# Transposing transfers from unit 3 on instead of unit 5, with a new hand-written order, in a fused gated-recurrence and MLP kernel

## The chip, the cores and the metric

The kernel runs on one core of one Trainium2 chip. The metric is device microseconds of one execution, median of three. All arithmetic is fp32. The engines are TensorE (PE, with its weight loads as PEld), VectorE (DVE), ScalarE (ACT), GpSimd (POOL) and SyncE (SP). SP issues most of the DMAs. [...]

## The reference

```python
def _attn_ref(q, k, v, f_logit):          # (B, H, S, D) = (4, 8, 768, 48)
    f = 1.0 / (1.0 + np.exp(-f_logit))
    state = np.zeros((B, H, D, D))
    for t in range(S):
        state = f[:, :, t, :, None] * state + einsum('bhd,bhe->bhde', k[:, :, t], v[:, :, t])
        y[:, :, t] = einsum('bhd,bhde->bhe', q[:, :, t], state)
    return y
def _moe_ref(x, g_ln, w_ch1, w_ch2):      # x: (4, 768, 384), heads side by side
    xn = (x - mean) / sqrt(var + 1e-6) * g_ln
    return x + maximum(xn @ w_ch1, 0.0) @ w_ch2      # 384 -> 1536 -> 384
```

The inputs q, k and v are normal with deviation 0.1. f_logit is normal with mean 2.0 and deviation 0.5, so a gate f is about 0.88.

## The kernel before

**Units.** The 768 positions are cut into NU = 12 units of T = 64. A unit holds all four batches and eight heads, 256 rows in all. Unit n first goes through attention and then through the MLP, and attention runs ahead of the MLP by one to three units. In attention a unit is turned so that a head's 48 channels lie on the partitions and its 64 positions along the free axis. ACT takes the sigmoid of f into `gates` (L674 to L684). Two scans on DVE then run the product of gates over the 64 positions, from the end (`after`, L652) and from the start (`upto`, L664). DVE multiplies k by `after` (kh) and q by `upto` (qh). PE makes the scores, the part carried from the state, the values, and the sum that goes into the next state (`chunk`).

**Two ways to turn a tile.** For n < DIRECT (5 before) the tiles of f, q, k and kh are turned by PE against the identity (`across` L640, `do_kt` L765), eight 128x128 transposes for each tensor, and ACT or DVE reads the result from PSUM. For n >= DIRECT three steps do it. `split` (L426) has ACT cut half a tile into two 16-bit planes and POOL issue its store to DRAM. `transfer` (L440) has SP issue a transposing DMA back. The turned f and the turned q land in the same tile, `turned`. The turned k lands in the tile that held raw q before. Raw q of such a unit is loaded into k's tile (`raw_of`, L417). `do_gates` (L679) then reads `turned` for f, and `do_q` (L715) reads `turned` for q.

**The order is text.** START is the order of the first units and UNIT is repeated for m = 3 to 11, with n = m+1, o = m+2, p = m+3 and z = m+4. `run` (L1035) carries out one token after another in the order written, and every engine's queue and every dependence between two accesses of a tile follows from it. The tokens:

- `a3.gates` and so on: one stage of attention of unit 3; a stage already done is passed over
- `m2`: the next step of unit 2's MLP
- `l4k`: load k of unit 4; `p4k0`: split half 0 of it; `x4k`: its transposing transfer. K is kh, whose transfer is issued by `a4.kt`
- `f`, `r`, `w`: fetch, read and write one piece of the weights, which arrive as 64-bit numbers
- `t`, `T`, `u`, `U`: mixtures of the weights on DVE or (capitals) POOL
- `d`: an idle matmul; `s2`, `y3`: sums that the MLP's fast matrix products need

**MLP.** Units 0 to 2 compute the first layer plainly (L956) and units 3 to 11 by a scheme of 15 block products (L894). Units 0 and 1 compute the second layer plainly (L966) and the others by seven products (L985).

**The check at the end.** `do_q` keeps in `least` (L717) the smallest product of gates over the 64 positions of any channel of any unit (`total`, L661, not below 1e-30). After UNIT of m = 9 the minimum is taken, and at m = 10 `small` is set to 1 if it lies under LEAST = 1e-12 (L1078). After the last unit every engine loads `small` into a register (L1083) and branches on it (L1084). If it is 1, `general_path` (L19 to L296) computes the entire output again from the inputs, without a division by products of gates. It is a loop over 4 batches, and in it a loop over 3 stretches of 256 positions. Each pass loads its four tensors in eight transfers, turns f, q and k by PE, builds the scores by seven doublings of a block (L153 to L187), each with 16 matmuls, two products in place and a predicated copy, and then runs its MLP plainly (36 and 24 matmuls of 256 and 384 columns). Nothing of one pass lies beside the next.

Of the kernel before, what the change touches and what calls it, by code (L numbers as in the profile page):

```python
# [8 lines left out]
FP32 = mybir.dt.float32  # L9
# [289 lines left out]


START = """
l0k a0.gates l0q f d d a0.after d r l0v a0.kx
a0.upto f a0.kept l1f a0.k l1k d a0.q f a0.carried a0.scores a0.causal
a0.values l1q w d r d a0.stats f a0.kt a1.gates w
a0.norm d a1.after l1v a0.chunk a0.turn f r a0.state a1.upto m0 d
a1.kept w a1.kx f a1.k m0 a1.q f r a1.kt r w
a1.carried d a1.scores a1.causal f l2k f l2v f w m0 a1.values
l2f r r a1.stats a1.chunk w m0 a1.norm m0 a1.turn r m0
m1 r w m1 r w w f l2q w m1
f m1 a1.state a2.gates a2.after r m1 a2.kx m0 m0 r w  # L310
a2.k l3k w a2.upto a2.kept m1 a2.q m0 m0 m0 a2.carried l3q
m0 a2.scores l3v a2.causal U m1 a2.values a2.stats l3f a2.norm m1
m1 m1 a3.gates m1 a2.kt m1 a2.turn a2.chunk a3.kx m2 l4f a3.after
U a3.k a3.upto U T m2 a2.state m2 a3.q a3.kept m2 a3.carried
a3.scores a3.kt U U l4v l4k a4.gates a3.causal U U U t
U a3.values a3.chunk l4q T l5v a4.after m2 l5f U a3.stats m2
a4.kx U l5k a3.norm s2 m2 p5f0 a3.state m2 a4.k U m2
p5f1 m2 a4.kt a3.turn u l6f x5f p5k0 a4.upto a4.q p5k1
y3 l5q a5.gates m2 m2 a4.kept m2
"""  # L320
UNIT = """
m{m} a{o}.after a{n}.kt m{m} a{n}.carried p{o}q0 a{n}.scores m{m} p{o}q1 a{n}.causal m{m} m{m}
l{p}k m{m} m{m} a{o}.upto a{n}.values x{o}q x{o}k m{m} a{n}.stats p{p}f0 p{p}f1 m{m}
m{m} a{n}.chunk m{m} a{n}.norm m{m} m{m} m{m} m{m} s{m} m{m} p{p}k0
p{p}k1 l{p}q m{m} a{o}.q m{m} x{p}f a{n}.turn a{o}.k l{p}v p{o}K0 a{p}.gates m{m}
a{n}.state l{z}f a{o}.kept m{m} y{n} m{m} m{m} p{o}K1
"""


# [1 line left out]
def kernel(  # L331
# [21 lines left out]
    P = 128  # L353
    T = 64
# [3 lines left out]
    NS = 2 * GA  # L358
# [8 lines left out]
    LEAST = 1e-12  # L367
    PLAIN = 2
    FIRST = 3
    DIRECT = 5  # L370
    PIECE = 768

    outer = ctx.enter_context(tc.tile_pool(name="outer", bufs=1))
# [10 lines left out]
    work = fast.enter_context(tc.tile_pool(name="work", bufs=1))  # L384
# [17 lines left out]
    for name, fill in (("f", 40.0), ("q", 0.0), ("k", 0.0)):  # L402
        t = consts.tile([P, G, H, 64], FP32, name=f"{name}raw")
# [7 lines left out]
    turned = {}  # L411
# [3 lines left out]
    def raw_of(n, name):  # L415

        return wide_heads["k" if n >= DIRECT and name == "q" else name]  # L417

# [7 lines left out]
    def split(n, name, g):  # L426

        if n >= NU or n < DIRECT:
            return
# [10 lines left out]
    def transfer(n, name):  # L440

        if n >= NU or n < DIRECT:
            return
        if not turned:
            turned["k"] = wide_heads["q"].rearrange("p g h e -> p (g h e)").rearrange(
                "p (s t) -> p s t", t=T)
            turned["f"] = turned["q"] = late["pool"].tile([P, NS, T], FP32, name="turned")
        transposed(turned[name].rearrange("p (g s) t -> p g (s t)", g=G), n, name)

    def transposed(dst, n, name):  # L450
        there = halved.pop((n, name))
        to = dst.rearrange("p g c -> p (g c)").bitcast(U16)
        nc.sync.dma_start_transpose(out=to.rearrange("p (a r) -> p a r", a=GA),
                                    in_=there.rearrange("p two g c -> (p two) (g c)"))
# [130 lines left out]
    late = {}  # L585
# [42 lines left out]
    def attention(n):  # L628
# [7 lines left out]
        def new(name, shape, **kw):  # L636
            at[name] = work.tile(shape, FP32, tag=name, name=f"{name}{n}", **kw)
            return at[name]

        def across(src, g):  # L640

            pt = one_bank(f"tr{n}")
            for a in range(NP):
                nc.tensor.transpose(pt[:, a * P:(a + 1) * P],  # L644
                                    src[:, g, 2 * a:2 * a + 2].rearrange("p h e -> p (h e)"),
                                    ident)
            return pt.rearrange("p (s t) -> p s t", t=T)
# [20 lines left out]
        def times(dst, pts, by):  # L668
            for g, pt in enumerate(pts):
                segs = slice(g * HS, (g + 1) * HS)  # L670
                nc.vector.tensor_tensor(out=dst[:, segs], in0=pt, in1=by[:, segs, 1:E1],
                                        op=ALU.mult)

        def do_gates():  # L674
            new("after", [P, NS, E1])
            new("upto", [P, NS, E1])
            new("total", [P, NS], bufs=2)
            if n >= DIRECT:
                nc.scalar.activation(out=gv[:, :, 1:E1], in_=turned["f"], func=AF.Sigmoid)  # L679
# [17 lines left out]
        def do_k_across():  # L697
            if n < DIRECT:
                at["pk"] = [across(loaded[n, "k"], g) for g in range(G)]

        def do_k():
            kh = new("kh", [P, NS, T])
            if n < DIRECT:
                times(kh, at["pk"], at["after"])
# [330 lines left out]
    def run(plan):  # L1035
        for token in plan.split():
            kind, rest = token[0], token[1:]
            if kind == "a":
                n, stage = rest.split(".")
                if int(n) >= NU:  # L1040
                    continue
                if "a" + n not in running:
                    running["a" + n] = attention(int(n))
                running["a" + n].pop(stage, bool)()
            elif kind == "m":
                if token not in running:
                    running[token] = mlp(int(rest))
                next(running[token])
            elif kind == "l":
                load(int(rest[:-1]), rest[-1])  # L1050
            elif kind == "p":
                split(int(rest[:-2]), rest[-2], int(rest[-1]))
            elif kind == "x":
                transfer(int(rest[:-1]), rest[-1])
            elif kind == "s":
                sums(int(rest))
            elif kind == "y":
                if FIRST <= int(rest) < NU:
                    sums_of_x(int(rest))
            else:  # L1060
                {"r": read, "w": write, "f": fetch, "t": mix, "d": idle,
                 "T": lambda: mix(nc.gpsimd), "u": mix_step,
                 "U": lambda: mix_step(nc.gpsimd)}[token]()
# [53 lines left out]
```

## Time and profile before

| | |
|---|---|
| median of three runs | 444.21 us (443.25 to 448.19) |
| the profiled execution | 446.42 us, its span 444.6 us |
| TensorE busy | 425.5 us (96%) |
| VectorE, ScalarE, GpSimd busy | 332.8, 201.7, 146.3 us |
| granted TensorE clock | 1.000 |
| transposing transfers | 28, four for each of units 5 to 11 |
| transposes of f, q, k, kh on PE | 160, 32 for each of units 0 to 4 |
| one repeated unit | about 33 us |

Busy time of each engine by stretch of the execution, in us:

| stretch | length | PE | DVE | ACT | POOL | DMA share |
|---|---|---|---|---|---|---|
| 0 to 26 | 26.0 | 16.11 | 19.78 | 10.44 | 8.23 | 0.95 |
| 26 to 100 | 74.0 | 72.24 | 55.71 | 31.51 | 26.59 | 0.68 |
| 100 to 150 | 50.0 | 49.96 | 35.81 | 18.66 | 29.45 | 0.53 |
| 150 to 183.5 | 33.5 | 33.50 | 28.23 | 18.01 | 10.41 | 0.75 |
| 217 to 250 | 33.0 | 33.00 | 27.32 | 18.78 | 11.14 | 0.85 |
| 412 to 445 | 33.0 | 28.08 | 13.22 | 6.83 | 3.11 | 0.09 |

A row is a stretch of the span, and a number is how long that engine had an instruction in work in it. Of the lines of `general_path` the trace holds no instruction.

### The profile page before, as it was taken

To read this page: it belongs to the slowest core of one execution; us is meant where nothing else is said; L and a number is where in the kernel's file an instruction comes from. 1 tells how busy PE (TensorE), PEld (TensorE's weight loads), DVE (VectorE), ACT (ScalarE), POOL (GpSimd) and SP (SyncE) were. 2 spreads that over 40 slices of the span, in tenths; PEclk is the share of its full clock that TensorE was granted. 3 is DMA by queue.
4 is the path that set the end of the run, shared out by engine and by line. 5 is a ranking of instruction groups with operands and counts; after the bars stand their busy time and mean duration, and the time that the engine had idled before them with its cause. 6 is when DMAs were issued, how large, how long until landed. Compare 5 with 4: busy or idle time off the path is not lost.

```text
span 444.6 us, 12876 instructions
## 1 busy us (share of the span) xinstructions
PE 425.5 (96%) x5427; PEld 393.0 (88%) x5427; DVE 332.8 (75%) x528; ACT 201.7 (45%) x345; POOL 146.3 (33%) x165
## 2 busy tenths in 40 slices
PE   5789999999999999999999999999999999999995
PEld 4567787667899999989999989989999999999995
DVE  5897979443878988878888878878888878566461
ACT  2456772013244556456456556556555444151320
POOL 2214444139815123323324323323324214102011
PEclk9999999999999999999999999999999999999999
DMA  8996893241737759897978897898988871400001
GB/s 139 205 230 211 211 249 76 53 91 37 130 60 151 175 98 217 197 158 205 201 128 230 207 192 163 199 194 167 204 190 160 180 148 43 111 1 19 20 2 39
DMA packets 175630, 63.29 MB, mean 142 GB/s; under 512 B 162512, under 2 KB 168144, under 8 KB 175568
## 3 DMA queue, kind: packets, MB, share of 16 engines
q1 hardware_dynamic: 169312, 47.34, 55.7%
q0 software_dynamic: 4480, 14.68, 9.7%
q8 instruction: 44, 0.72, 0.7%
q10 hardware_dynamic: 1776, 0.40, 0.5%
q14 instruction: 18, 0.15, 0.1%
HBM read 28.31 MB, written 19.40 MB: 107 GB/s over the span
## 4 chain that ended last, share of the span: by engine, by line
PE 83%; DVE 6%; DMA 4%; issue 3%; POOL 2%; SPq 1%; ACT 1%; POOLq 0%; ACTq 0%
PE pp L985 28%; PE ph L956 11%; PE bx L894 10%; PE by L894 7%; PE po L966 7%; DMA kt<-Khalves 3%; PE bz L894 3%; PE shared L750 3%; PE py L736 2%; PE tr L644 2%; PE py L778 2%; PE shared L809 2%; PE bv L894 2%; PE bw L894 2%; PE xp L842 2%
## 5 line engine op out<-in xcount | busy, mean ns | idle before, releaser
L905 ACT ACTIVATE h<-h 128x512 f32<-128x512 f32 x45 | 28.1, 630 | 52.2 <-DVE h L902 48.0
L956 PE MATMUL ph<-xt,w 128*128 128x256 f32 x216 | 48.7, 381 | 0.6 <-ACT xt L844 0.6
L956 PEld LDWEIGHTS ph<-xt,w 128*128 128x128 f32 x216 | 40.3, 190 | 6.3 <-issue 0.8
L985 PE MATMUL pp<-mixed,h 128*128 128x192 f32 x240 | 42.4, 327 | 0.0
L985 PE MATMUL pp<-mixed,s 128*128 128x192 f32 x240 | 42.0, 326 | 0.0
L985 PE MATMUL pp<-w,h 128*128 128x192 f32 x240 | 40.7, 326 | 0.0
L985 PEld LDWEIGHTS pp<-mixed,h 128*128 128x128 f32 x240 | 39.5, 190 | 0.3 <-ACT xt L844 0.3
L985 PEld LDWEIGHTS pp<-mixed,s 128*128 128x128 f32 x240 | 39.1, 190 | 0.0
L985 PEld LDWEIGHTS pp<-w,h 128*128 128x128 f32 x240 | 38.8, 190 | 0.0
L993 POOL TENSOR_TENSOR p1x<-p,x 128x192 f32<-128x192 f32 x10 | 13.1, 1312 | 66.5 <-ACT p L1000 66.5
L902 DVE TENSOR_TENSOR h<-h,bx 128x512 f32<-128x512 f32 x27 | 18.6, 687 | 21.1 <-PE bx L894 21.1
L966 PE MATMUL po<-w,h 128*128 128x384 f32 x96 | 32.4, 489 | 0.0
L652 DVE TENSOR_TENSOR_SCAN after<-gates,ends 128x1040 f32<-128x1040 f32 (+1 forms) x13 | 29.1, 2236 | 4.0 <-ACT gates L684 3.3
L797 POOL TENSOR_SCALAR rstd<-mv 128x2 f32<-128x2 f32 x12 | 3.1, 261 | 84.6 <-DVE mv L796 84.6
L664 DVE TENSOR_TENSOR_SCAN upto<-gates,starts 128x1040 f32<-128x1040 f32 (+1 forms) x13 | 30.0, 2305 | 0.4
L844 ACT ACTIVATE xt<-xp,gain 128x128 f32<-128x128 f32 x72 | 20.1, 375 | 21.1 <-PE xp L842 21.0
L894 PE MATMUL bx<-y,v 128*128 128x128 f32 x216 | 29.4, 279 | 0.0
L902 DVE TENSOR_TENSOR h<-h,by 128x512 f32<-128x512 f32 x36 | 24.5, 682 | 5.2 <-PE by L894 5.0
L966 PEld LDWEIGHTS po<-w,h 128*128 128x128 f32 x96 | 17.7, 190 | 11.0
L894 PEld LDWEIGHTS bx<-y,v 128*128 128x128 f32 x216 | 26.2, 192 | 0.5
L958 ACT ACTIVATE h<-ph 128x512 f32<-128x512 f32 x18 | 10.8, 597 | 29.5 <-PE ph L956 29.4
L556 POOL TENSOR_TENSOR w<-w_0upper,w_0units 128x768 int32<-128x768 int32 x7 | 12.7, 1818 | 30.7 <-DVE w_0upper L554 26.3
(162 smaller groups left out, 954.0 us busy)
## 6 DMA issues: line engine op xcount, KB each, us to landing
w_0words<-in_moe_w_ch_dram SPq DMA_DIRECT2D x7, 768.0 KB, 6.3
kraw<-in_k_dram SPq DMA_DIRECT2D x48, 96.0 KB, 3.8
v<-in_v_dram SPq DMA_DIRECT2D x48, 96.0 KB, 3.8
fraw<-in_f_logit_dram SPq DMA_DIRECT2D x46, 96.0 KB, 3.5
fhalves<-fplanes POOLq DMA_DIRECT2D x14, 256.0 KB, 5.3
khalves<-kplanes POOLq DMA_DIRECT2D x14, 256.0 KB, 3.5
qhalves<-qplanes POOLq DMA_DIRECT2D x14, 256.0 KB, 3.5
Khalves<-Kplanes POOLq DMA_DIRECT2D x14, 256.0 KB, 3.5
```

The lines of the kernel that those rows point to most:

```text
L556: nc.gpsimd.tensor_tensor(out=to.bitcast(I32), in0=upper, in1=units, op=ALU.add)
L652: nc.vector.tensor_tensor_scan(out=at["after"].rearrange(flat)[:, c0:c1][:, ::-1], data0=gt[:, c0 + 1:c1 + 1][:, ::-1], data1=ends.rearran ...
L664: nc.vector.tensor_tensor_scan(out=at["upto"].rearrange(flat)[:, c0:c1], data0=gt[:, c0:c1], data1=starts.rearrange(flat)[:, c0:c1], initi ...
L750: nc.tensor.matmul(ps[half(b), r, e], lhsT=kh[head_rows(r), seg], rhs=qh[head_rows(r), seg], start=True, stop=True)
L844: nc.scalar.mul(out=xt[:, m, g * P:(g + 1) * P], in_=pt[:, m], mul=gain[:, m:m + 1])
L894: nc.tensor.matmul(banks[bank][:, i], lhsT=right[:, i * P:(i + 1) * P], rhs=left, start=new and i == 0, stop=True, skip_group_check=True)
L902: nc.vector.tensor_tensor(out=out[to], in0=out[to], in1=bank, op=op)
L905: nc.scalar.activation(out=out[to], in_=out[to] if bank is None else bank, func=AF.Relu)
L956: nc.tensor.matmul(ph[:, j], lhsT=w1[:, m, (i + j) * P:(i + j + 1) * P], rhs=xt[:, m], start=m == 0, stop=m == KD - 1)
L966: nc.tensor.matmul(po, lhsT=h[:, i, g * P:(g + 1) * P], rhs=w2[:, i], start=i == 0, stop=i == KF - 1)
L985: nc.tensor.matmul(pp, lhsT=a[:, i], rhs=b[:, i], start=i == 0, stop=i == KH - 1)
L993: engine.tensor_tensor(out=to, in0=x1, in1=x2, op=op)
```

## The change

DIRECT becomes 3, so f, q, k and kh of units 3 and 4 are split and transferred as well. START gets the splits and transfers of units 3 and 4 (sixteen `p`, six `x` and two transfers in `a3.kt` and `a4.kt`) and loses `a3.kx`, `a4.kx` and `a4.kt`, of which the last is now done in UNIT. Both orders are new. The tile `turned` comes from another pool, since it is needed before the later pool exists.

```diff
 START = """
-l0k a0.gates l0q f d d a0.after d r l0v a0.kx
-a0.upto f a0.kept l1f a0.k l1k d a0.q f a0.carried a0.scores a0.causal
-a0.values l1q w d r d a0.stats f a0.kt a1.gates w
...
-m1 m1 a3.gates m1 a2.kt m1 a2.turn a2.chunk a3.kx m2 l4f a3.after
-U a3.k a3.upto U T m2 a2.state m2 a3.q a3.kept m2 a3.carried
-a3.scores a3.kt U U l4v l4k a4.gates a3.causal U U U t
-U a3.values a3.chunk l4q T l5v a4.after m2 l5f U a3.stats m2
-a4.kx U l5k a3.norm s2 m2 p5f0 a3.state m2 a4.k U m2
-p5f1 m2 a4.kt a3.turn u l6f x5f p5k0 a4.upto a4.q p5k1
-y3 l5q a5.gates m2 m2 a4.kept m2
+a0.upto a0.after f l0k d d a0.gates l0q l0v r d a0.kx f l1f a0.kept a0.k l1k d d a0.q f
+a0.scores a0.causal a0.carried f a0.kt l1q w a0.values r d d a0.stats a1.gates f w
...
+a2.gates a2.after m1 a2.kx m0 r m0 w a2.k l3f r w l3k a2.upto a2.kept m1 m0 p3f0 p3f1
+a2.q m0 m0 x3f a2.carried p3k1 l3q p3k0 a2.scores m1 l3v a2.causal a2.values a2.stats
+a3.gates a2.norm m1 l4f m1 U p3q1 a3.after p3q0 x3k a2.kt m0 U x3q a2.chunk p4f0 a2.turn
+a3.upto a3.k a3.q m1 m1 p4f1 U p3K1 l4k m2 U T x4f a2.state m2 p3K0 m2 p4k0 p4k1 a3.kept
+U m2 m1 a3.carried U p4q0 a3.scores U U a3.kt a3.causal a4.gates p4q1 t a3.values T U m2
+a4.after a3.chunk l5f U a3.stats x4k a3.state m2 l4q s2 U m2 l5k a3.norm l4v x4q a4.upto
+p5f0 m2 U p5f1 a4.k a3.turn l6f m2 a4.q x5f p5k0 p5k1 l5q m2 y3 m2 a4.kept m2 l5v
+a5.gates p4K0 u p4K1 m2
 """
 UNIT = """
-m{m} a{o}.after a{n}.kt m{m} a{n}.carried p{o}q0 a{n}.scores m{m} p{o}q1 a{n}.causal m{m} m{m}
-l{p}k m{m} m{m} a{o}.upto a{n}.values x{o}q x{o}k m{m} a{n}.stats p{p}f0 p{p}f1 m{m}
-m{m} a{n}.chunk m{m} a{n}.norm m{m} m{m} m{m} m{m} s{m} m{m} p{p}k0
-p{p}k1 l{p}q m{m} a{o}.q m{m} x{p}f a{n}.turn a{o}.k l{p}v p{o}K0 a{p}.gates m{m}
-a{n}.state l{z}f a{o}.kept m{m} y{n} m{m} m{m} p{o}K1
+m{m} a{o}.after m{m} a{n}.carried a{n}.scores a{n}.causal m{m} m{m} m{m} p{o}q0 m{m}
+p{o}q1 m{m} a{n}.values a{n}.kt l{p}k m{m} p{p}f0 x{o}q a{o}.upto m{m} m{m} x{o}k
+a{n}.stats m{m} m{m} p{p}f1 m{m} m{m} a{n}.chunk a{n}.state l{p}v m{m} a{n}.norm s{m}
+p{p}k0 a{o}.kept a{o}.k m{m} a{p}.gates m{m} a{n}.turn l{z}f p{p}k1 l{p}q m{m} a{o}.q
+x{p}f m{m} p{o}K0 m{m} p{o}K1 y{n} m{m} m{m}
 """
-    DIRECT = 5
+    DIRECT = 3
-            turned["f"] = turned["q"] = late["pool"].tile([P, NS, T], FP32, name="turned")
+            turned["f"] = turned["q"] = work.tile([P, NS, T], FP32, name="turned")
```

Three positions in the new order, for what they read. In the new UNIT `a{p}.gates` stands ahead of `x{p}f` and `a{o}.q`; in the old one it stood behind both. In START `l3q` stands between `p3k1` and `p3k0`, and all three use k's tile. `l4q` stands behind `p4q0` and `p4q1`, and all three use k's tile.

More of the change, by code (lines that the diff above doesn't have):

```diff
@@ L301 @@
 START = """
-l0k a0.gates l0q f d d a0.after d r l0v a0.kx
-a0.upto f a0.kept l1f a0.k l1k d a0.q f a0.carried a0.scores a0.causal
-a0.values l1q w d r d a0.stats f a0.kt a1.gates w
[L305 to L311, printed above, removed]
@@ L312 @@
-m0 a2.scores l3v a2.causal U m1 a2.values a2.stats l3f a2.norm m1
-m1 m1 a3.gates m1 a2.kt m1 a2.turn a2.chunk a3.kx m2 l4f a3.after
-U a3.k a3.upto U T m2 a2.state m2 a3.q a3.kept m2 a3.carried
-a3.scores a3.kt U U l4v l4k a4.gates a3.causal U U U t
-U a3.values a3.chunk l4q T l5v a4.after m2 l5f U a3.stats m2
-a4.kx U l5k a3.norm s2 m2 p5f0 a3.state m2 a4.k U m2
-p5f1 m2 a4.kt a3.turn u l6f x5f p5k0 a4.upto a4.q p5k1
-y3 l5q a5.gates m2 m2 a4.kept m2
+a0.upto a0.after f l0k d d a0.gates l0q l0v r d a0.kx f l1f a0.kept a0.k l1k d d a0.q f
@@ new lines @@
+a0.scores a0.causal a0.carried f a0.kt l1q w a0.values r d d a0.stats a1.gates f w
+a0.norm a1.after d a1.upto d l1v a0.chunk l2f f f a0.turn r a0.state m0 r a1.kx a1.kept
+w f a1.k m0 f a1.q r l2k f w a1.kt a1.carried a1.scores a1.causal l2v m0 a1.values r r w
+a1.stats a1.chunk w m0 a1.norm m0 a1.turn r m0 r m1 m1 l2q w r w w f m1 w m1 f a1.state
+a2.gates a2.after m1 a2.kx m0 r m0 w a2.k l3f r w l3k a2.upto a2.kept m1 m0 p3f0 p3f1
+a2.q m0 m0 x3f a2.carried p3k1 l3q p3k0 a2.scores m1 l3v a2.causal a2.values a2.stats
```

## The prediction

> **What bounds the kernel now.** The first view is the page's busy times, the second its chain of waits: TensorE carries both.
>
> ```profile
> PE 425.5 (96%) x5427; PEld 393.0 (88%) x5427; DVE 332.8 (75%) x528; ACT 201.7 (45%) x345; POOL 146.3 (33%) x165
> ...
> PE 83%; DVE 6%; DMA 4%; issue 3%; POOL 2%; SPq 1%; ACT 1%; POOLq 0%; ACTq 0%
> ```
>
> The third view is the list of waits, whose numbers are total, times and longest:
>
> ```profile
> PE shared L809 <- DMA kt<-Khalves: 2.9, 3, 1.1
> ```
>
> PE is idle for 444.6 - 425.5 = 19.1 us: about 10 ahead of 26 us, 5 at the end, 2.9 in this line (the state's products wait three times for kh's transfer). As long as the same instructions run, little but PE work can be won.
>
> So the fourth view asks whether the same instructions run: the lines of the check at the end, and the tiles `turned` and `least` (durations in ns: least, median, most; then first and last start).
>
> ```profile
> L1084 PEldq COMPARE_BRANCH  x1: 3498/3498/3498, 437.6 to 437.6; - x1
> L1084 DVEq COMPARE_BRANCH  x1: 72/72/72, 440.7 to 440.7; - x1
> ...
> L717 DVE TENSOR_TENSOR least<-least,total x12: 157/164/712, 14.5 to 373.3; 128x16 f32<-128x16 f32 x12
> ...
> L679 ACT ACTIVATE gates<-turned x7: 1058/1058/1061, 148.2 to 349.3; 128x1024 f32<-128x1024 f32 x7
> ```
>
> All engines reach the branch of L1084 within the last 10 us, and no line of the general path has an instruction: it was passed over. The branch hangs on `least`, which hangs on what `gates` read from `turned`, a tile that f and q share. The new order changes that.
>
> [...] PE's branch took 3498 ns, DVE's 72. [...] the eight k transposes at 9.74 us took 1.91 us, the eight of q at 12.11 us 1.04. [...] 32 score matmuls on tiles of 48x64 took 0.95 us. [...]
>
> **The change, part by part.**
>
> *1. `a{p}.gates` ahead of `x{p}f`.* In the old UNIT the transfer of f of unit p stands ahead of the sigmoid that reads it. In the new one the last write of `turned` ahead of `a{p}.gates` is `x{o}q`. So for p = 6 to 11 ACT takes the sigmoid of unit o's q, and the f that lands later is read by nobody. As q is about 0.1 in size, each such gate is about 0.5, and a product over 64 is about 0.5^64 = 5e-20. Worked out from the inputs, the smallest product of true gates is 8.2e-6 and the largest of sigmoid(q) is 2.8e-19. The limit is 1e-12, which is a mean gate of 0.649. All `a{o}.q` up to o = 11 stand ahead of the minimum at m = 9, so `small` becomes 1 and **the general path runs after the fast one**. It computes the entire output anew, whatever the fast part left.
>
> *2. The general path's price.* Nothing of it is in the trace, so I follow one pass along its dependences with the nearest rows.
> - Loads: a transfer of 64 rows by 8 heads is 0.67 us of SP (four take 2.64 to 2.68). Here it is 128 rows, so about 1.34. f, q and k are six, 8.0 us, and the last lands 3.1 us later (3.8 from issue less 0.67): 11.
> - k's turn: four transposes 0.53, a copy 0.60: 12.3.
> - Diagonal: the first 8 score matmuls 0.9 (a block product has 4 in 0.89; two row halves at once), [...] and q times gates at 1.21: 17.
> - Seven doublings: 16 matmuls between 0.9 us (64 columns streamed) and 1.75 [...], I take 1.6; two products at 0.69; 0.3 for hand-overs: 3.3 each. The predicated copy of 1024 (1.2) lies under the next matmuls; if it costs double, DVE sets 3.7. In all 23 (20 to 26): 40.
> - kh's eight transposes 1.04 and copy 0.59, 48 matmuls of 48 columns with the state's update between them about 6.5, the copy of x 0.8: 9, so 49.
> - Norm: statistics 2 x (0.54 + 0.18), POOL 0.26 + 0.77, two products at 0.72, six transposes and six ACT copies 2: 6, so 55.
> - MLP: 12 matmul records of 256 columns are 2.59 in the chain, so layer one is 6 x 2.59 = 15.5, plus 0.6; layer two has 24 matmuls at 2.59/4, 15.5: 87.
> - Add 0.55 and store about 2.5: 90. The loop's end: the trace has no loop. I take PE's 3.5 of the branch, between 0 and twice that: 94.
> - Clock: [...] Between 0 and 20 us if all of attention ran at half clock; I take 6.
>
> That is 100 us a pass (85 to 120), and nothing hides it, since the passes are one after the other. Twelve passes: 1200 us. Around them are the entry (two memsets of 2048 elements by the row of 1040 at 0.93, masks on POOL, a branch: about 10) and four outer rounds (about 4 each): 26. In all about 1226, with 1040 and 1470 as ends.
>
> *3. The fast part.* Units 3 and 4 lose 4 x 8 transposes each; eight take 1.04 at full clock, so 8.3 us of PE go. In their place ACT gets 16 splits at 1.05 and loses four kh copies at 0.59 (the sigmoid costs 1.06 instead of 2 x 0.60): about +14 us between 100 and 165, where it is busy for 18.66 of 50, so PE's work hides it. POOL gets 16 issues at 0.69, 11 us, in a stretch where it is busy for 29.45 of 50; behind them are the weight mixtures that unit 3's MLP reads. SP gets eight transposing transfers at 2.0 to 3.5, some 19 us, past which the loads of units 4 and 5 wait. DVE reads k and q from SBUF in one piece (1.21 for 2 x 0.68): -0.3 us a unit. In UNIT `p{o}K0` and `p{o}K1` stand two MLP steps further from the end (1.95 each), so kh lands earlier and the 2.9 us of waits go. A new wait: `p3k0` reads k's tile behind `l3q`, so ACT stands until that load lands (3.8 us); behind it are unit 2's copies of x and unit 1's and 0's MLP copies, which PE feels after four PSUM banks: 0 to 4 us. `p4q0` and `p4q1` stand ahead of `l4q` and take k again: no wait and no cost, only k's numbers in q's place. Weights are fetched ahead of k of unit 0 (768 KB in 6.3 us): k and q may land up to 1 us late; set against it `a0.kt` fills PE's 1.35 us wait for the causal product. Sum: 446.4 - 8.3 - 2.9 + (0 to 12), taking 4: 439; between 435 and 452. The profiled execution is 2.2 above the median of 444.2, so on the median's scale about 437.
>
> *Sum:* 437 + 1226 = 1663; I say **1665**.
>
> **The rivals.**
> - *General path at half clock in attention* (likely in part): +14 a pass on my 6, so 12 x 114 + 26 + 437 = 1831. For it: PE is busy for half of a doubling only. Against: from 12 to 26 us of this trace PE had gaps and stayed at full clock (eight transposes 1.04).
> - *Passes with cheaper hand-overs and shorter loads*: 85 a pass, 1020 + 20 + 437 = 1477. For it: hand-overs in this trace are under 0.1 us. [...]
> - *The branch is not taken* (the other side): then only part 3 counts, 437, about 1.6% faster; the 8.3 us of transposes on PE decide it. It decides where the least product is over 1e-12, and 5e-20 is far from that; it needs the sigmoid to see f although the transfer is written later in the order. In this form the change doesn't do what it says in either case: q of unit 4 is never split, and f of units 6 to 11 never read.
> - *Branch not taken and POOL or SP become the bound between 100 and 165*: 452 or more, 2% slower.
>
> **How the numbers follow.** General path taken: 0.96, of which about 0.6 lies within 1560 to 1760, 0.25 above (half clock, a dear loop end), 0.15 below. Not taken: 0.03 faster, 0.01 within 1% or slower. A change of under 1% could not be told from none here. Range: 1480 to 1900, the ends of the pass at about 86 and 120; the cases outside it are the 4% without the branch and the tails, some 0.2. Faster 0.03, same 0.01, slower 0.96.
>
> **What would show it.** Instructions on L117 to L284, twelve repetitions behind some 437 us; `gates` reading `turned` without a wait for `fhalves`; PE's share falling to about a half and its busy time rising by about 12 x 50; 96 transposes of units 0 to 2 in the fast part instead of 160, and 36 transposing transfers instead of 28. A span near 440 without those lines would prove part 1 wrong. A pass of 85 or 120 would show which row of part 2 was mis-sized: loads, doublings, or loop end.

## The result, and the profile after

The changed kernel takes 1773.06 us (median of 4 runs, 1765.98 to 1775.46), against 445.49 us before. The ratio is 3.976 (95% interval 3.949 to 4.004). The forecast was 1665 us (1480 to 1900), slower. Where some executions of a version took over 1.5% longer than its fastest, its ratio rests on the others alone, which matters for moved_mix, of whose six runs three (458.92 to 463.90 us) are left out.

First the page of the changed kernel: busy times, then the busy tenths of PE and its granted clock in 40 slices of 44 us each.

```profile
span 1773.8 us, 27959 instructions
...
PE 1420.9 (80%) x11483; PEld 1220.6 (69%) x11483; DVE 672.3 (38%) x976; ACT 354.7 (20%) x619; POOL 201.8 (11%) x310
...
PE   7997999999677786777857778677786877868678
...
PEclk9998999999558585575865758558585675856858
```

Ten slices are the kernel as one knows it. Then come thirty in which PE's digits lie between 5 and 8 and its clock swings between 0.5 and a little over 0.8. There are more than twice as many instructions as before.

The second view is the check at the end and the loops behind it (durations in ns as least, median, most; then first and last start in us).

```profile
L1079 PEldq COMPARE_BRANCH  x1: 90/90/90, 445.8 to 445.8; - x1
...
L289 PEldq COMPARE_BRANCH  x20: 87/223/327, 446.6 to 1770.9; - x20
...
L72 SPq DMA_DIRECT2D gfraw<-in_f_logit_dram x24: 383/410/432, 450.8 to 1664.1; - x24
```

PE comes to the branch at 445.8 us and goes on into the general path, which was passed over before. There f is loaded from 450.8 us to 1664.1, two transfers in each of twelve passes. From one pass's first load to the next lie 110.2 us on average (108.3 to 111.9).

The third view is the tile `gates`: the sigmoid that writes it, and what released it when it had to wait. The first fence is the changed kernel and the second the kernel before.

```profile
L674 ACT ACTIVATE gates<-turned x9: 1057/1058/1062, 91.5 to 346.2; 128x1024 f32<-128x1024 f32 x9
...
its engine sat idle before it (us, times) until:
  DMA turned<-fhalves: 12.9, 1
  DMA turned<-qhalves: 9.1, 5
```

```profile
its engine sat idle before it (us, times) until:
  DMA turned<-fhalves: 24.3, 7
```

Before, the sigmoid waited for f's transfer seven times, once in each of units 5 to 11. Now it waits for f in unit 5 only, and for **q's** transfer in five of the six units 6 to 11; for unit 7 q had landed already. The order is the same in all six. For unit 6, the transfer of unit 5's q into `turned` is issued at 173.4 us, the sigmoid starts at 180.6, and unit 6's f is issued at 192.2. So what the sigmoid reads there is q. That this is what calls the general path is for the experiments to show.

The last view is the chain of PE in one pass of the general path.

```profile
672.71 2.35 PE L117 MATMUL gtr<-ident,gfraw 128*128 128x128 f32 x8 [7.91 <-DMA gfraw<-in_f_logit_dram]
...
679.83 3.79 PE L143 MATMUL gpd<-gz 48*128 48x128 f32 x32
686.24 3.68 PE L164 MATMUL gpl<-gz 48*128 48x64 f32 x32 [2.62 <-DVE gz L149]
691.40 3.68 PE L164 MATMUL gpl<-gz 48*128 48x64 f32 x32 [1.48 <-DVE gz L175]
...
741.75 17.80 PE L270 MATMUL gph<-gxt,w 128*128 128x256 f32 x72 [0.59 <-ACT gxt L263]
759.39 15.64 PE L277 MATMUL gpo<-w,gh 128*128 128x384 f32 x48
```

A line is start, duration, instructions, and in brackets the idle time before them with its releaser. A doubling is 5.2 us long: 3.7 us of matmuls and 1.5 us in which PE waits for DVE's two products. The two MLP layers at the end are half as long as the attention ahead of them.

### The profile page after: what moved, and what is told of

The parts are those of the page before. It is cut to its first block, busy times and chain, and to the rows that moved or that the text cites. A ratio compares the mean times of both kernels' runs of the same rounds, so it can differ in the third digit from the quotient of the medians.

```text
span 1773.8 us, 27959 instructions
## 1 busy us (share of the span) xinstructions
PE 1420.9 (80%) x11483; PEld 1220.6 (69%) x11483; DVE 672.3 (38%) x976; ACT 354.7 (20%) x619; POOL 201.8 (11%) x310
## 5 line engine op out<-in xcount | busy, mean ns | idle before, releaser
L164 PE MATMUL gpl<-gz 48*128 48x64 f32 (+1 forms) x2688 | 286.9, 402 | 142.9 <-DVE gz L175 109.8
L164 PEld LDWEIGHTS gpl<-gz 48*128 48x128 f32 (+1 forms) x2688 | 273.7, 311 | 156.9 <-issue 156.9
L270 PE MATMUL gph<-gxt,w 128*128 128x256 f32 x864 | 219.8, 423 | 7.1 <-ACT gxt L263 7.1
L270 PEld LDWEIGHTS gph<-gxt,w 128*128 128x128 f32 x864 | 184.9, 216 | 42.0 <-ACT gxt L263 11.9
L277 PE MATMUL gpo<-w,gh 128*128 128x384 f32 x576 | 187.7, 486 | 0.0
L175 DVE TENSOR_TENSOR gz<-gz,ggates 128x512 f32<-128x512 f32 x168 | 108.7, 689 | 194.0 <-issue 149.3
L277 PEld LDWEIGHTS gpo<-w,gh 128*128 128x128 f32 x576 | 109.6, 190 | 73.6
L181 DVE COPY_PREDICATED gscores<-gmask,gpl 128x1024 f32<-128x1024 int32 x72 | 118.4, 1644 | 0.0
L203 PE MATMUL gpy<-gv,gscores 128*128 128x48 f32 x384 | 87.6, 416 | 0.0
L203 PEld LDWEIGHTS gpy<-gv,gscores 128*128 128x128 f32 x384 | 83.7, 331 | 2.2
```

What stands on the lines that cost most here:

```text
L164: nc.tensor.matmul(plv[0:m, par, c, a].rearrange("s (n h) -> s n h", h=half), lhsT=z[rows, 1, a, c * C:c * C + m], rhs=late, start=True, s ...
L175: nc.vector.tensor_tensor(out=zz, in0=zz, op=ALU.mult, in1=pv[:, i].broadcast_to([P, nblk, half]))
L181: nc.vector.copy_predicated(out=sc.rearrange("s i (n two h) -> s two i n h", two=2, h=half)[:, 1], mask=masks[half].rearrange("s (o n h) - ...
L203: nc.tensor.matmul(py[:, par, at:at + D], lhsT=scv[:, par, c, a], rhs=vt[:, c, 2 * a + par], start=c == 0 and a == 0, stop=False, skip_gro ...
L270: nc.tensor.matmul(ph[:, j], lhsT=w1[:, m, (i + j) * P:(i + j + 1) * P], rhs=xt[:, m], start=m == 0, stop=m == KD - 1)
L277: nc.tensor.matmul(po, lhsT=h[:, i, c * C:(c + 1) * C], rhs=w2[:, i], start=i == 0, stop=i == KF - 1)
```

## The experiments

### The branch, and what it costs

**fast_only** is the changed kernel with another limit:

```diff
-    LEAST = 1e-12
+    LEAST = 1e-25
```

> The changed kernel with the limit LEAST at 1e-25 in place of 1e-12; the sigmoid still reads q in place of f in units 6 to 11, and the general path is left out if the limit alone decides. My theory (the branch on the smallest gate product runs the general path): the branch is passed over, because 5e-20 lies above 1e-25, and the time is the fast part's, which in the trace of the changed kernel ended 8.3 us later than before (448.3 against 440.1): 454 us, 450 to 458. Rival (the general path runs for another reason than gates near 0.5): 1770 us as before the edit. Rival (the fast part itself is faster than before, and the trace of the changed kernel stretched it): 437 us.

It took 453.41 us (ratio to before 1.018, interval 1.012 to 1.024). The general path is gone by the limit alone, so it was the gate products that called it: the smallest lies between 1e-25 and 1e-12. Units 6 to 11 still work with gates taken from q. The rest is the fast part, 453 us, and slower than before.

**forced_before** is the kernel before with `LEAST = 1e-5`.

> The kernel before with LEAST at 1e-5, just above its own smallest gate product of 8.2e-6, and nothing else. My theory (the general path is a fixed price on top of any fast part): 445 + 1319 = 1764 us, 1750 to 1780, with passes of 110 us and the granted clock at 0.5 in attention. Rival (what the general path costs depends on what the changed fast part left behind, such as transfers still in flight): away from 1764 by over 20 us. If my reading of the limit were wrong: 445.

It took 1754.53 us (ratio 3.934, interval 3.911 to 3.958), with passes of 106.6 to 111.1 us. So the general path costs about 1310 us on top of the kernel before and about 1320 on top of the changed fast part (1773 - 453). It is in the main a price of its own. The passes average 109.4 us here and 110.2 in the changed kernel, which over twelve makes the 10 us between the two; why they differ by 0.9 us was not looked into.

### Which token calls it

**unit_asis** has START and DIRECT = 5 as before and the new repeated unit untouched.

> START and DIRECT = 5 as before, and the new repeated unit exactly as in the change. My theory: a{p}.gates ahead of x{p}f alone brings the general path: 445 + 1310 = 1750 us, 1735 to 1775. Rival (the general path needs the new START too): 440 to 450.

It took 1764.14 us (ratio 3.954, interval 3.928 to 3.979). The new START isn't needed for the slowdown.

**only_gates** moves one token of the changed kernel:

```diff
-p{p}k0 a{o}.kept a{o}.k m{m} a{p}.gates m{m} a{n}.turn l{z}f p{p}k1 l{p}q m{m} a{o}.q
-x{p}f m{m} p{o}K0 m{m} p{o}K1 y{n} m{m} m{m}
+p{p}k0 a{o}.kept a{o}.k m{m} m{m} a{n}.turn l{z}f p{p}k1 l{p}q m{m} a{o}.q
+x{p}f m{m} p{o}K0 m{m} p{o}K1 a{p}.gates y{n} m{m} m{m}
```

> The changed kernel with one token moved: a{p}.gates stands behind x{p}f and p{o}K1 in the repeated unit. START is as changed, so q of unit 4 and half of k of unit 3 hold other numbers. My theory: this one position decides, the general path is gone, and the time is that of the fast part, 454 us (448 to 460), a few us more if the sigmoid now waits for f's transfer. Rival (other positions of the new order also bring gate products under the limit): 1770.

It took 488.78 us (ratio 1.097, interval 1.091 to 1.104). The general path is gone, so this position decides. But 454 was wrong by 35 us. Against fast_only, PE's waits for the copies of the next unit's first products (`h`) rose from 0.7 to 24.3 us, and the same 5363 records of PE kept it busy for 437.0 us instead of 424.4. The next runs show how.

### What the change costs when each stage reads its own tensor

**repaired** also puts `p3k0` ahead of `l3q`, and `l4q` behind `p4k1`, ahead of `p4q0`.

> The changed kernel with three tokens moved so that each split and each sigmoid reads its own tensor: a{p}.gates behind x{p}f, p3k0 ahead of l3q, l4q ahead of p4q0. This is what the change says it does. My blind sum of part 3: 437 us on the median's scale, 1.6% faster than before (435 to 452). What the trace of the changed kernel says in its place: PE waits 6.5 us for the norm of unit 3 and 2.5 us for a copy behind it, and the fast part ends 8.3 us later: 452 us, 1.5 to 2% slower. p3k0 no longer waits for l3q's load, which takes 6.8 us off ACT's waits but nothing off PE's.

It took 488.84 us (ratio 1.097, interval 1.091 to 1.103): both expectations missed. Its list of waits (total, times, longest) says why.

```profile
ACT gates L674 <- DMA turned<-fhalves: 68.6, 7, 11.5
...
DVE after L647 <- ACT gates L674: 44.7, 7, 8.6
...
PE bx L889 <- ACT h L894: 23.8, 7, 5.2
```

This is one wait handed on. `x{p}f` stands at the unit's end, because `turned` is free only once `a{o}.q` has read q. A sigmoid close behind it waits up to 11.5 us. Behind the sigmoid ACT's queue holds the copies of the next unit's first products, and PE waits for those, up to 5.2 us in a unit. The timeline of ACT and of PE in one unit shows it:

```profile
277.34 1.06 ACT L674 ACTIVATE gates<-turned 128x1024 f32<-128x1024 f32 x1 [11.46 <-DMA turned<-fhalves]
278.30 0.58 ACT L894 ACTIVATE h<-bw 128x512 f32<-128x512 f32 x1
```

```profile
279.42 2.07 PE L889 MATMUL bx<-y,w 128*128 128x128 f32 x8 [5.16 <-ACT h L894]
281.29 1.92 PE L889 MATMUL by<-y,w 128*128 128x128 f32 x8
282.99 1.51 PE L889 MATMUL bx<-xt,v 128*128 128x128 f32 x8
284.34 1.06 PE L889 MATMUL by<-xt,v 128*128 128x128 f32 x8
```

After the gap of 5.2 us PE's products run slow for about 5 us (2.07 against 1.06), so this gap cost more than its length. Repaired takes as long as only_gates, so the two misplaced loads in START (`l3q` and `l4q`) cost nothing that can be seen.

The two halves of the order were then taken apart. **unit_only** has START and DIRECT = 5 as before and the repeated unit of repaired:

> START and DIRECT = 5 as before, and the new repeated unit with a{p}.gates behind x{p}f. My theory (the wait for f's transfer at the unit's end costs PE about 4 to 5 us in each of the units in which it happens, six or seven): 470 to 482 us. Rival (START makes the loss): 445.

It took 482.56 us (ratio 1.081, interval 1.075 to 1.087), just past the 470 to 482 expected. **start_only** has START of repaired, DIRECT = 3 and the old repeated unit:

> The new START with p3k0 ahead of l3q and l4q ahead of p4q0, DIRECT = 3, and the old repeated unit, in which f's transfer stands ahead of the sigmoid. My theory: the 35 us that the repaired kernel loses against the fast part alone come from the new repeated unit, where the sigmoid waits 11.5 us for a transfer put at the unit's end; with the old unit what is left is START: 64 transposes of 8.3 us off PE against some 12 us of new PE waits for the norm of unit 3, 445 to 455 us. Rival (the transfers themselves, eight more of them, bring the loss through SP and the DMA engines): 470 to 490. Rival (blind sum of part 3, less the repeated unit's 2.9 us of waits that go): 440.

It took 458.57 us (ratio 1.029, interval 1.024 to 1.034), 3.6 us past the upper end of my theory and far below the rival of 470 to 490. So the new unit, with `a{p}.gates` where I put it, costs about 36 us (no run put it elsewhere behind `x{p}f`), and the new START with two more units transferred about 12. Most of what START loses is seen in the stretch from 100 to 150 us (columns: length, busy us of PE, PEld, DVE, ACT and POOL with counts, clock, DMA share, GB/s). First the kernel before, then start_only:

```profile
100.00:150.00 50.00, 49.96 (x581) 44.31 (x580) 35.81 (x54) 18.66 (x37) 29.45 (x27) 1.00 0.53 110
```

```profile
100.00:150.00 50.00, 41.14 (x457) 34.28 (x447) 36.62 (x36) 20.27 (x35) 32.94 (x32) 0.93 0.82 170
```

PE has 124 records fewer, which includes transposes that went, but it stands for 9 us, and its mean clock falls to 0.93. In the next 33 us it stands for another 4.9 us. The waits of PE (total, times, longest) of start_only, and the wait for the norm in fast_only and in the kernel before:

```profile
PE shared L804 <- DMA kt<-Khalves: 9.1, 5, 3.6
PE xp L837 <- DVE xn L827: 5.4, 3, 3.9
```

```profile
PE xp L837 <- DVE xn L827: 11.8, 3, 9.0
```

```profile
PE xp L842 <- DVE xn L832: 1.2, 1, 1.2
```

The longest wait for kh's transfer (3.6 us) and the longest for a norm (3.9 and 9.0 us, the norm of unit 3) lie in that stretch. On DVE, ahead of that norm, fast_only shows this, and the kernel before the line below it:

```profile
123.95 5.01 DVE L574 TENSOR_TENSOR mixed<-w 128x384 f32<-128x384 f32 x1
```

```profile
L579 DVE TENSOR_TENSOR mixed<-w x2: 547/548/550, 125.0 to 126.1; 128x384 f32<-128x384 f32 x2
```

The same instruction takes 0.55 us while POOL is idle and 5.0 us beside POOL's mixtures. The four of them together take 8.9 us in place of 2.2. From 124 to 135 us POOL works in fast_only without a gap, and its instructions beside the one of 5.01 us take 0.96 to 1.52 us each, so 5.0 us is more than a wait for one of them. How POOL's work stretches DVE's is not shown. No run changes this overlap alone, so that it makes the norm late is argued from the timelines and not shown.

### A version without these queues

**moved_start** changes start_only by a few tokens:

```diff
-a3.upto a3.k a3.q m1 m1 p4f1 U p3K1 l4k m2 U T x4f a2.state m2 p3K0 m2 p4k0 p4k1 l4q a3.kept
+a3.upto a3.k a3.q m1 m1 p4f1 U p3K1 p3K0 l4k m2 x4f a2.state a3.kt U T m2 m2 p4k0 p4k1 l4q a3.kept
-U m2 m1 a3.carried U p4q0 a3.scores U U a3.kt a3.causal a4.gates p4q1 t a3.values T U m2
+U m2 m1 a3.carried U p4q0 a3.scores U U a3.causal a4.gates p4q1 t a3.values m2
-a4.after a3.chunk l5f U a3.stats x4k a3.state m2 s2 U m2 l5k a3.norm l4v x4q a4.upto
+a4.after a3.chunk l5f a3.stats T x4k a3.state m2 a3.norm s2 U U U m2 l5k l4v x4q a4.upto
```

> start_only (458.6 us) with a few tokens of START moved: p3K0 beside p3K1 and a3.kt ahead of the mixtures U T, so that POOL issues kh's stores and SP its transfer before 5 us of mixtures; T and three U behind a3.stats, so that POOL's part of unit 3's norm does not queue behind them; a3.norm ahead of s2 on DVE. My theory (PE's waits for kh's transfer of 3.6 us and for the norm of 3.9 us, and the half clock behind them, are POOL's queue): 6 to 10 us go, 449 to 453 us. Rival (the queue is only the nearest of several causes, and DVE's sums or SP are late next): 455 to 459. To beat the kernel before it must be under 445.

The time is 456.4 us and the ratio 1.022 (1.016 to 1.028): it overlaps with start_only's, so a gain isn't shown, and my theory missed. Slow products stood behind one of its two waits only: in start_only 12 records of 256 columns took 4.71 us behind the wait of 3.6 us, and 2.86 ahead of it; behind the wait of 3.9 us 24 records of 192 columns took 4.07, as against 4.06 ahead of it. The waits for kh's transfer shrank to 0.4 us, and in their place stand 2.8 us for DVE's sums and 2.7 for DVE's last additions. That is the rival's case.

**moved_mix** puts all mixtures of the second layer on DVE, where it idles, and the scan of unit 4 behind the sums:

> moved_start (456.5 us) with the mixtures of the second layer's weights, two of three of which were on POOL and one ahead of unit 3's statistics on DVE, all on DVE in its idle time behind a3.k and a3.kept, and with a4.after behind the sums s2. My theory (after the queue of POOL the queue of DVE ahead of unit 3's statistics and sums is what PE waits for between 120 and 145 us: mixtures that take up to 5 us beside POOL's, and the scan of unit 4): the 2.8 us wait for the sums and the waits for the norm go, 448 to 453 us. To beat the kernel before it must be under 445; by the 8.3 us of transposes on PE 440 would be the end of it. Rival (unit 4's scan is late next, and its transfers with it): 455 to 462.

The time is 451.72 us, as expected, and the ratio 1.014 (1.008 to 1.020): better than start_only as far as three runs can say, yet slower than before. PE's longest waits are now 2.6, 2.6, 2.3 and 2.2 us, each with another releaser. No version with DIRECT = 3 that was tried reached the kernel before. Which of its waits would have to go for that stays open.

### The clock in the general path

**forced_fill2** and **forced_fill4** add idle matmuls to forced_before, behind the 16 matmuls of each doubling, two or four:

```diff
+            for _ in range(2):
+                nc.tensor.matmul(one_bank("gidle")[:, 0:2 * P], lhsT=ident,
+                                 rhs=ident.unsqueeze(1).broadcast_to([P, 2, P]), start=True, stop=True)
```

> The kernel before with LEAST at 1e-5, so that the general path runs (1754 us), and two idle matmuls of 256 columns on 128 rows behind the 16 matmuls of every doubling. It asks what holds attention's clock at 0.5. If the clock follows PE's activity and the idle matmuls add enough: the 16 matmuls fall from 3.68 to 1.84 us, a doubling from 5.21 to about 3.4, twelve passes of seven doublings lose 150 us: 1600 us (1560 to 1640). If the clock stays at 0.5: the idle matmuls take 1.84 us where PE waits 1.53, so about +0.3 us a doubling, 1780 us.

> The kernel before with LEAST at 1e-5 and four idle matmuls in place of two behind the 16 matmuls of every doubling. With two, PE was busy for 98% of the doublings and its clock still stayed at 0.5 for 35 us. If the clock follows how many columns stream through the array, and not how long PE is busy: four idle matmuls make half of PE's time dense, the clock goes to 1.0 early, a doubling takes 1.84 + 1.72 = 3.6 us instead of 5.2 and the time is 1620 us (1590 to 1680). If the clock stays at 0.5 for another reason: 3.68 + 3.7 = 7.4 us a doubling, about 1930 us.

They took 1736.91 and 1662.46 us, against 1754.53 without. The first lies between its two cases and fits neither; the second lies in the range of its first case. The doublings of one pass, first with two and then with four idle matmuls:

```profile
567.11 3.68 PE L164 MATMUL gpl<-gz 48*128 48x64 f32 x32 [2.62 <-DVE gz L149]
570.72 2.07 PE L169 MATMUL gidle<-ident 128*128 128x256 f32 x4
572.72 3.68 PE L164 MATMUL gpl<-gz 48*128 48x64 f32 x32
```

```profile
568.60 3.78 PE L169 MATMUL gidle<-ident 128*128 128x256 f32 x8
572.31 2.17 PE L164 MATMUL gpl<-gz 48*128 48x64 f32 x32
574.41 1.99 PE L169 MATMUL gidle<-ident 128*128 128x256 f32 x8
576.33 2.00 PE L164 MATMUL gpl<-gz 48*128 48x64 f32 x32
```

With two, PE is busy for 32.9 of the 35 us from 565 to 600, and its clock there is 0.50. With four, it is busy for 34.8 of 35 and the clock is 0.89. A doubling falls from 5.2 to 3.9 us although PE does more. So attention's half clock makes the pass longer, and over these 35 us four idle matmuls lifted it and two did not. That it follows from how long PE is busy alone, forced_fill2 does not bear out. What sets it is not shown: the matmuls of a doubling have 64 columns on 48 rows, and the idle ones 256 on 128.

## Why the prediction was right, and where its sums were off

**The cause was right.** Part 1 said that ACT takes the sigmoid of unit o's q, that `small` becomes 1, and that the general path runs behind the fast one. The releaser of the sigmoid, the branch, fast_only, only_gates and unit_asis show each link. Of the signs named, the twelve repetitions are there, behind 448 us instead of 437, and so are the 36 transposing transfers and the 96 transposes of units 0 to 2. The sign for PE was off: it is busy for 80% of the span and not about a half, and its busy time rose by 83 us a pass and not 50. Half clock makes some 20 of these 33 us, by the estimate below.

**The price of a pass was 110, not 100 us, and the term that was mis-sized is the clock.** By the steps of part 2, predicted against the pass from 669.2 to 781.1 us (the longest of the eleven intervals; a round of the outer loop ends in it):

| step | predicted | measured |
|---|---|---|
| loads and turn | 12.3 | 10.7 |
| diagonal | 4.7 | 6.4 |
| seven doublings | 23 | 34.6 |
| kh, values, state, copy | 9 | 15.6 |
| norm | 6 | 5.2 |
| MLP, 15.5 + 15.5 + 0.6 | 32 | 33.3 |
| add, store, loop end | 7 | 6.1 |
| clock | 6 | in the rows above |

Loads and turn, norm, MLP and the end are each within 2 us of the guess. The diagonal, the doublings and the values took 20 us more, and for the clock I had 6 of a range of 0 to 20. That these 20 us are the clock follows from the same instructions where they ran fast. In forced_fill4 the 16 matmuls of a doubling took 2.00 us instead of 3.68, and in forced_fill2 a group of the values 1.99 instead of 3.65; over all such rows of a pass but the diagonal that makes 18 us, an estimate from these traces. The rival "general path at half clock in attention" had 114 a pass and was the nearer one. What spoke against it was that PE stayed fast over gaps between 12 and 26 us of the trace of before (eight transposes in 1.04 us at 12.11 us and again at 18.72). In the passes it did not: the clock was 0.50 from 669 to 742 us and 0.95 in the MLP behind.

Three details of part 2. The 16 matmuls of a doubling were put, by estimate, between 0.9 and 1.75 us; at the faster clock of forced_fill4 they took 2.00, past that end. Weight loads did lie beside matmuls in the trace of before: 24 matmul records of L985, on all 128 rows, take 4.07 us from 426.26 us on, and 24 weight loads of 128 rows, 3.88 us together, run beside them. What the predicated copies cost was the author's estimate: two of 512 took 1.33 us together, twice in the diagonal. One of 1024 took 1.24 us in four doublings and 2.43 in the first two (the seventh has a copy on ACT instead); all six lie under the next matmuls, as predicted. PE's branch at the loop's end took 0.22 us in the median, not 3.5. The branch over the general path does take PE 3.50 us where it is taken (before) and 0.09 where it is not (the changed kernel), but what those 3.50 us are spent on is in no trace. The row of the loop's end is near its guess only because drains, semaphores and register work, which it did not count, lie between 778.2 and 781.1 us.

**The fast part was 453, not 437 us,** just past its stated end of 452. Part 3 took 4 us for new waits, of 0 to 12. The 8.3 us of transposes did go: those instructions were busy for 23.5 us before and for 15.2 in the changed kernel's fast part. But in fast_only PE stood for 8.1 us more than before, with 9 us for unit 3's norm behind stretched mixtures on DVE, and its busy time fell by 1.1 us only (425.5 to 424.4). That the rest of the 8.3 us went into slow stretches after gaps (clock 0.93 from 100 to 150 us; 24 records of 192 columns took 4.90 us behind the gap of 9 us and 4.06 ahead of it) is likely and was not tested. The stretching of DVE's mixtures beside POOL's (8.9 us for four, 2.2 before) was not in the sum at all. It was also wrong to let `p3k0`'s wait cost PE something: ACT stood for 6.8 us, and without that wait, in repaired, the time is the same as in only_gates.

The sum, as the prediction itself said, stood for a kernel that does not do what the change says. With each stage reading its own tensor the changed orders take 488.8 us (repaired), 52 more than the 437 of part 3, and part 3 had no term for the wait of the sigmoid, because in the changed kernel the sigmoid of units 6 to 11 does not wait for f.

**The entry was 2, not 26 us**: the masks and memsets lie beside the first loads, and the outer rounds are in the 110.

The errors partly cancel in 1665 against 1773: +16 for the fast part, 12 x 10.2 = +122 for the passes, -24 for the entry. That makes 114 where 108 were missing; the rest is not assigned. The one cancellation, of the entry, is luck, and a small one.

## What to carry to other kernels

Before a reordered kernel is costed, follow each tile that two values share, and ask which write each read sees in the new order. An order that turns a read-after-write into a write-after-read looks cheaper than it is, because the wait is gone; here the same order costs 35 us more once the read waits for its own data. Where a kernel has a guard with a slow path, the guard's operands belong to the change: a trace that shows the path untaken has no price for it, and it can be the whole result. And in a kernel that fills TensorE, as this one does, 8.3 us of work taken off it did not pay, because waits behind other queues grew; a gap cost its length and, behind the one of 5.2 us, a slow stretch of 5 us after it.

## What was not expected of the hardware

- In forced_fill2 PE was busy for 94% of 35 us at a clock of 0.50, with matmuls of 64 columns in which two idle ones of 256 follow every 16. With four idle ones (forced_fill4) it was 0.89. In forced_fill2's pass PE did get faster at last: two idle matmuls took 1.15 us behind the seventh doubling and 2.07 behind the six ahead, and eight matmuls of the values, of 48 columns, ran in 1.99 us and eight more, 1 us later, in 3.65 again.
- One DVE subtraction of 128x384 took 0.55 us with POOL idle (before, 125.0 us) and up to 5.01 us with POOL at work beside it (fast_only, 123.95 us).
